# A channel-attention kernel: freed rows of maxima refilled with x, graded last loads, stores in more pieces, another order of reloads

## The chip, the cores and the metric

The kernel runs on one core of one Trainium2 chip; the other cores are idle. The metric is the device time of one execution in microseconds (us), lower is better. A profiled execution also has a span, from its first to its last instruction, about 1.8 us shorter than its time. Medians are over the executions of a kernel.

Engines are named as the profile names them: PE is TensorE, DVE is VectorE, ACT is ScalarE, SP is SyncE. Here SP issues all loads of x and ACT all stores. A "row" below means 128 x 384 bf16 values, one row of 384 channels in each of 128 partitions: 98,304 bytes.

## The reference

```python
# x: (1, 384, 384, 384) bf16; w1: (384, 96); w2: (96, 384)
xf = x.reshape(B, H * W, C)
gap = jnp.mean(xf, 1)                  # mean of each channel over all pixels
gmp = jnp.amax(xf, 1)                  # maximum of each channel over all pixels
h_a = relu(gap @ w1)                   # relu written out for this page
h_m = relu(gmp @ w1)
scale = sigmoid(h_a @ w2 + h_m @ w2)
return x * scale[:, None, None, :]
```

The scale of a channel needs all of x, and the output needs the scale. So x (113.25 MB, 1152 rows) is read once for the sums and maxima, and read again for the product, but for what can stay on the chip.

## The kernel before

The first pass streams x through six slots of SBUF. TensorE adds up the rows, VectorE keeps an accumulator of 11 rows of maxima. When all of x has passed, the last six blocks are still in their slots, and the first 16 rows lie in PSUM. Those 277 rows are not read again.

```python
SLOTS = (44, 44, 44, 44, 44, 41)       # rows in each slot: 261
PSUM_ROWS = 16
ACC_ROWS = 11
HALVES, QUARTERS = 9, 4                # last blocks: nine loaded in halves, four in quarters
FIRST_STORES = ((1, 2, 3, 4, 4, 6, 8, 8, 8), (10, 12, 22))
...
loads = [(0, PSUM_ROWS, 0, 0, PSUM_ROWS)]
for i, (first, n, s) in enumerate(blocks):
    behind = n_blocks - 1 - i
    j = 0
    for m in cut(n, 4 if behind < QUARTERS else 2 if behind < QUARTERS + HALVES else 1):
        loads.append((first, n, s, j, j + m))
        j += m
...
for i, (first, n, s, lo, hi) in enumerate(loads):          # the first pass
    rows = slots[s][:, lo:hi, :]
    m = hi - lo
    nc.sync.dma_start(out=rows, in_=rows_of(xr, first, n)[:, lo:hi, :])
    ...                                                     # sums on TensorE
    for j in range(0 if i else A, m, A):
        k = min(A, m - j)
        nc.vector.tensor_tensor(out=acc[:, 0:k, :], in0=acc[:, 0:k, :], in1=rows[:, j:j + k, :], op=ALU.max)
```

Then comes the turn between the passes: the 11 rows of maxima are halved to one, transposed, reduced, and put through the two small matrix products and the sigmoid.

```python
n = A
while n > 1:
    h = n // 2
    nc.vector.tensor_tensor(out=acc[:, 0:h, :], in0=acc[:, 0:h, :], in1=acc[:, n - h:n, :], op=ALU.max)
    n -= h
...
nc.scalar.activation(out=scale_bc, in_=z_ps, func=ACT.Sigmoid)
```

In the second pass VectorE multiplies a block in its slot, ACT issues its store, and SP reloads the slot with a block of the rest when the store has landed.

```python
while k < len(order):
    first, n, s = order[k]
    pieces = list(firsts.pop(0)) if firsts else [n]
    put(order[k], pieces)              # multiply and store, piece by piece
    k += 1
    fits = [b for b in again if b[1] <= SLOTS[s]]
    if fits:
        ...
        get(b, cut(b[1], 2) if k <= 2 else [b[1]])
        order.append(b)
```

## Time and profile before

| | before |
|---|---|
| median of the first 6 executions | 747.89 us (747.2 to 756.33) |
| span of the profiled one | 746.1 us |
| bytes moved | 312.81 MB |
| last load's bytes end / first store's bytes begin | 268.7 us / 279.1 us |
| halving of the maxima begins / scale ready | 272.0 us / 277.8 us |

From the page of the kernel before. The busy line has one digit for each fortieth of the span, in tenths; the GB/s line is what the transfer engines moved in the same slices. The queue lines give packets, MB and the time of their packets as a share of 16 engines over the span; q1 carries the loads, q10 the stores.

```profile
span 746.1 us, 2405 instructions
...
DMA  9999999999999939999999999999999999999997
GB/s 382 427 430 434 424 435 431 421 428 430 425 429 419 421 159 369 435 433 435 429 450 427 429 435 435 432 424 434 445 435 435 435 423 432 433 437 432 437 424 341
DMA packets 16363, 312.81 MB, mean 419 GB/s; under 512 B 2176, under 2 KB 2528, under 8 KB 4320
...
q1 hardware_dynamic: 10368, 199.27, 62.6%
q10 hardware_dynamic: 5984, 113.40, 35.5%
```

The transfer engines are full except in slice 15, which is the turn, and at the very end. Everything else hides behind them.

The turn, from the timeline of VectorE before. Columns: start and length in us, engine, line, operation, output and inputs, count; in brackets the idle time before it and what ended it.

```profile
263.06 8.94 DVE L153 TENSOR_TENSOR acc<-acc,x_90 128x4224 bf16<-128x4224 bf16 x4
272.03 2.74 DVE L168 TENSOR_TENSOR acc<-acc 128x1920 bf16<-128x1920 bf16 x4
275.43 0.56 DVE L172 TENSOR_REDUCE gT<-bank_a 128x3 bf16<-128x384 bf16 x1 [0.67 <-PE bank_a L171]
276.41 0.29 DVE L175 TENSOR_SCALAR hbc<-bank_a 96x128 bf16<-96x128 f32 x1 [0.42 <-PE bank_a L174]
277.81 9.51 DVE L181 TENSOR_TENSOR x_85<-x_85,scale_bc 128x384 bf16<-128x384 bf16 x9 [1.12 <-ACT scale_bc L177]
```

VectorE goes from the last maxima into the halving without idle time: it is behind the loads. The same stretch in windows (busy time and count of each engine, PE clock, share of the transfer engines, GB/s):

```profile
268.00:269.00 1.00, 0.64 (x8) 0.26 (x2) 1.00 (x1) 0.26 (x1) 0.00 (x0) 0.50 0.32 131
269.00:272.00 3.00, 1.95 (x8) 1.69 (x9) 2.96 (x2) 0.79 (x3) 0.00 (x0) 0.50 0.00 0
272.00:275.00 3.00, 1.95 (x37) 1.47 (x38) 2.63 (x4) 0.45 (x2) 0.00 (x0) 0.50 0.00 0
...
279.00:280.00 1.00, 0.00 (x0) 0.00 (x0) 1.00 (x2) 0.00 (x0) 0.00 (x0) 0.50 0.70 247
```

No byte moves from 269 to 279 us. That is the dead time the change aims at.

The cost of a maximum, from VectorE's groups by form (busy us, mean ns of one, idle before):

```profile
L153 DVE TENSOR_TENSOR acc<-acc,x_85 128x4224 bf16<-128x4224 bf16 x16 | 37.7, 2358 | 2.4 <-DMA x_85<-in_x_dram 1.9
...
L168 DVE TENSOR_TENSOR acc<-acc 128x1920 bf16<-128x1920 bf16 x1 | 1.2, 1159 | 0.0
```

Eleven rows take 2.358 us and five 1.159, so a row costs 0.200 us and an instruction 0.160 us besides. The Trainium skill, "VectorE: DVE Perf Modes", section "The TRN2 errata", says that operations on SBUF pay a fixed cost per instruction, measured there at about 150 cycles of 0.96 GHz; 0.160 us are 153 cycles, so this trace agrees. A piece cut so that it needs one more instruction costs VectorE that much more.

### The profile page before, as it was taken

The numbers are of one execution on the slowest core, as the hardware profiler recorded it, in microseconds if no ns is written. First come the engines' busy times: TensorE is split into PE (matmuls) and PEld (weight loads), VectorE is DVE, ScalarE is ACT, GpSimd is POOL, SyncE is SP. The second block draws the span as 40 slices with busy tenths as digits, with TensorE's granted clock in tenths as the row PEclk, the third lists the DMA queues.
The fourth block names the chain that finished last, engine by engine and source line by source line (L and its number), as shares of the span: only waits on it lengthen the run. The fifth ranks groups of instructions, "written<-read, shape, count | busy, mean of one in ns | idle before, by whom it ended". The sixth has DMA issues, their size and how long they took to land.

```text
span 746.1 us, 2405 instructions
## 1 busy us (share of the span) xinstructions
PE 127.6 (17%) x949; PEld 40.4 (5%) x949; DVE 488.5 (65%) x158; ACT 3.5 (0%) x9; POOL 0.7 (0%) x6
## 2 busy tenths in 40 slices
PE   1554433445445540000000000000000000000000
PEld 0111111111111120000000000000000000000000
DVE  4989999999999989997444434444434444444420
ACT  0000000000000010000000000000000000000000
POOL 0000000000000000000000000000000000000000
PEclk9766766755555555555555555555555555555555
DMA  9999999999999939999999999999999999999997
GB/s 382 427 430 434 424 435 431 421 428 430 425 429 419 421 159 369 435 433 435 429 450 427 429 435 435 432 424 434 445 435 435 435 423 432 433 437 432 437 424 341
DMA packets 16363, 312.81 MB, mean 419 GB/s; under 512 B 2176, under 2 KB 2528, under 8 KB 4320
## 3 DMA queue, kind: packets, MB, share of 16 engines
q1 hardware_dynamic: 10368, 199.27, 62.6%
q10 hardware_dynamic: 5984, 113.40, 35.5%
q8 instruction: 7, 0.11, 0.1%
q14 instruction: 4, 0.03, 0.0%
HBM read 199.41 MB, written 113.25 MB: 419 GB/s over the span
## 4 chain that ended last, share of the span: by engine, by line
another core or an unknown queue 42%; DMA 28%; DVE 24%; SPq 1%; DVEq 1%; issue 0%; PE 0%; ACT 0%
DVE acc L153 21%; DMA x_87<-in_x_dram 9%; DMA x_89<-in_x_dram 7%; DMA out_dram<-x_89 6%; DMA w_sb<-in_w_dram 3%; DMA out_dram<-x_86 2%; DVE x_85 L181 1%; DVE x_86 L181 1%; DMA x_86<-in_x_dram 1%; SPq L199 1%; DVEq L245 1%; DVE acc L168 0%; DVE gT L172 0%; PE bank_a L171 0%
## 5 line engine op out<-in xcount | busy, mean ns | idle before, releaser
L181 DVE TENSOR_TENSOR x_85<-x_85,scale_bc 128x16896 bf16<-128x16896 bf16 (+6 forms) x13 | 45.3, 3537 | 36.2 <-DMA x_85<-in_x_dram 35.1
L181 DVE TENSOR_TENSOR x_86<-x_86,scale_bc 128x16896 bf16<-128x16896 bf16 (+4 forms) x7 | 44.3, 6354 | 33.7 <-DMA x_86<-in_x_dram 32.4
L181 DVE TENSOR_TENSOR x_87<-x_87,scale_bc 128x16896 bf16<-128x16896 bf16 (+1 forms) x5 | 37.4, 7476 | 37.1 <-DMA x_87<-in_x_dram 37.1
L181 DVE TENSOR_TENSOR x_89<-x_89,scale_bc 128x16896 bf16<-128x16896 bf16 x4 | 35.8, 8956 | 32.5 <-DMA x_89<-in_x_dram 32.5
L181 DVE TENSOR_TENSOR x_88<-x_88,scale_bc 128x16896 bf16<-128x16896 bf16 x4 | 35.8, 8956 | 31.7 <-DMA x_88<-in_x_dram 31.7
L181 DVE TENSOR_TENSOR x_90<-x_90,scale_bc 128x15744 bf16<-128x15744 bf16 x4 | 33.4, 8356 | 31.0 <-DMA x_90<-in_x_dram 31.0
L153 DVE TENSOR_TENSOR acc<-acc,x_89 128x4224 bf16<-128x4224 bf16 x20 | 47.2, 2358 | 6.5 <-DMA x_89<-in_x_dram 5.9
L115 PEld LDWEIGHTS <-ones_bf 128*1 128x1 bf16 x900 | 36.5, 111 | 231.2 <-issue 228.3
L153 DVE TENSOR_TENSOR acc<-acc,x_90 128x4224 bf16<-128x4224 bf16 (+3 forms) x20 | 44.2, 2208 | 0.8
L153 DVE TENSOR_TENSOR acc<-acc,x_85 128x4224 bf16<-128x4224 bf16 (+1 forms) x17 | 38.9, 2287 | 2.4 <-DMA x_85<-in_x_dram 1.9
L153 DVE TENSOR_TENSOR acc<-acc,x_88 128x4224 bf16<-128x4224 bf16 (+1 forms) x17 | 39.3, 2311 | 1.5 <-DMA x_88<-in_x_dram 1.0
L153 DVE TENSOR_TENSOR acc<-acc,x_86 128x4224 bf16<-128x4224 bf16 x16 | 37.7, 2358 | 2.6 <-DMA x_86<-in_x_dram 2.1
L153 DVE TENSOR_TENSOR acc<-acc,x_87 128x4224 bf16<-128x4224 bf16 x16 | 37.7, 2358 | 1.4 <-DMA x_87<-in_x_dram 0.9
L115 PE MATMUL bank_a<-x_89,ones_bf 128*1 128x512 bf16 (+2 forms) x171 | 24.5, 600 | 30.2 <-DMA x_89<-in_x_dram 30.2
L115 PE MATMUL bank_a<-x_85,ones_bf 128*1 128x512 bf16 (+1 forms) x150 | 20.8, 588 | 30.9 <-DMA x_85<-in_x_dram 30.9
L115 PE MATMUL bank_a<-x_88,ones_bf 128*1 128x512 bf16 (+2 forms) x144 | 20.4, 590 | 20.9 <-DMA x_88<-in_x_dram 20.9
L115 PE MATMUL bank_a<-x_90,ones_bf 128*1 128x512 bf16 (+3 forms) x159 | 19.3, 523 | 20.8 <-DMA x_90<-in_x_dram 20.8
L115 PE MATMUL bank_a<-x_86,ones_bf 128*1 128x512 bf16 (+1 forms) x138 | 18.9, 587 | 22.5 <-DMA x_86<-in_x_dram 22.5
L115 PE MATMUL bank_a<-x_87,ones_bf 128*1 128x512 bf16 (+2 forms) x138 | 18.5, 566 | 20.8 <-DMA x_87<-in_x_dram 20.8
L149 DVE COPY acc<-x_85 128x4224 bf16<-128x4224 bf16 x1 | 1.3, 1260 | 5.6 <-DMA x_85<-in_x_dram 5.6
L155 DVE COPY kept_ps<-x_85 128x3072 uint32<-128x3072 uint32 x1 | 3.4, 3355 | 0.0
L181 DVE TENSOR_TENSOR x_88<-kept_ps,scale_bc 128x6144 bf16<-128x6144 bf16 x1 | 3.4, 3351 | 0.0
(33 smaller groups left out, 18.4 us busy)
## 6 DMA issues: line engine op xcount, KB each, us to landing
x_89<-in_x_dram SPq DMA_DIRECT2D x6, 4224.0 KB, 34.3
x_85<-in_x_dram SPq DMA_DIRECT2D x5, 4224.0 KB, 34.4
x_87<-in_x_dram SPq DMA_DIRECT2D x5, 4224.0 KB, 34.9
x_88<-in_x_dram SPq DMA_DIRECT2D x5, 4224.0 KB, 34.7
x_90<-in_x_dram SPq DMA_DIRECT2D x5, 3936.0 KB, 34.2
x_86<-in_x_dram SPq DMA_DIRECT2D x4, 4224.0 KB, 36.0
out_dram<-x_87 ACTq DMA_DIRECT2D x4, 4224.0 KB, 74.4
out_dram<-x_88 ACTq DMA_DIRECT2D x4, 4224.0 KB, 73.6
```

The lines of the kernel that those rows point to most:

```text
L115: nc.tensor.matmul(sum_ps[q * QP:q * QP + 1, 0:g * P], lhsT=ones_bf[:, 0:1], rhs=rows[:, k:k + g, q * P:(q + 1) * P], start=(done + k == 0 ...
L149: nc.vector.tensor_copy(out=acc, in_=rows[:, 0:A, :])
L153: nc.vector.tensor_tensor(out=acc[:, 0:k, :], in0=acc[:, 0:k, :], in1=rows[:, j:j + k, :], op=ALU.max)
L155: nc.vector.tensor_copy(out=kept_ps.bitcast(U32), in_=rows.bitcast(U32))
L181: nc.vector.tensor_tensor(out=dst, in0=src, in1=scale_bc.unsqueeze(1).to_broadcast([P, n, C]), op=ALU.mult)
L199: nc.sync.dma_start(out=slots[s][:, j:j + m, :], in_=rows_of(xr, first, n)[:, j:j + m, :])
L245: with _tile.TileContext(nc) as tc:
```

## The change

Its intent: use the dead time and shorten it. Ten of the 11 rows of maxima are spent after the halving; they are filled with x in the turn, so that ten rows fewer are streamed later. Two small tiles are laid over others, which makes room for two more rows in the last slot. The last loads get smaller towards the end, so that less work follows the last of them. The first blocks are stored in more pieces, and the first reload is to wait until two blocks are stored.

```diff
-SLOTS = (44, 44, 44, 44, 44, 41)
+SLOTS = (44, 44, 44, 44, 44, 43)
-HALVES, QUARTERS = 9, 4
-FIRST_STORES = ((1, 2, 3, 4, 4, 6, 8, 8, 8), (10, 12, 22))
+LAST_LOADS = ((22, 22),) * 7 + ((17, 16, 11), (17, 16, 11), (15, 15, 14), (11, 11, 11, 11), (10, 9, 8, 8, 8))
+FIRST_STORES = ((1, 2, 3, 4, 4, 6, 8, 8, 8), (8, 8, 9, 9, 10), (10, 12, 22))
+FIRST_READS = (2, 2)
+LEAD = 2
+ACC_STORES_AT = 3
...
-    left = TOT - PSUM_ROWS
+    head = PSUM_ROWS + A - 1
+    left = TOT - head
...
-    w2_sb = consts.tile([R, C], BF16)
+    scale_bc = consts.tile([P, C], BF16)
+    w2_sb = scale_bc[0:R, :]
+    s_sb = consts.tile([P, P], F32)
+    hbc = s_sb[0:R, :].bitcast(BF16).rearrange("r (t p) -> r t p", t=2)
...
-    loads = [(0, PSUM_ROWS, 0, 0, PSUM_ROWS)]
+    loads = [(0, PSUM_ROWS, 0, 0, PSUM_ROWS), (PSUM_ROWS, A - 1, 1, 0, A - 1)]
...                                     # pieces of the last blocks now from LAST_LOADS
     while n > 1:
         h = n // 2
         nc.vector.tensor_tensor(out=acc[:, 0:h, :], in0=acc[:, 0:h, :], in1=acc[:, n - h:n, :], op=ALU.max)
         n -= h
+        if n > 1 and acc_pieces:
+            continue
+        lo, hi = n, acc_pieces[0][0] if acc_pieces else A
+        nc.sync.dma_start(out=acc[:, lo:hi, :], in_=rows_of(xr, PSUM_ROWS, A - 1)[:, lo - 1:hi - 1, :])
+        acc_pieces.append((lo, hi))
...                                     # put() multiplies and stores acc after three pieces
+        if k == LEAD:
+            read_into(order[k - 1][2])
+            for j in range(k - 1):
+                read_into(order[j][2])
+        elif k > LEAD:
+            read_into(order[k - 1][2])
```

More of the change, by code (lines that the diff above doesn't have):

```diff
@@ L59 @@
         n = min(SLOTS[slot], left)
-        blocks.insert(0, [left - n + PSUM_ROWS, n, slot])
+        blocks.insert(0, [left - n + head, n, slot])
         left -= n
@@ L79 @@
     nc.scalar.dma_start(out=w1_sb, in_=w1.rearrange("(q p) m -> p q m", p=P))
-    w2_sb = consts.tile([R, C], BF16)
+    scale_bc = consts.tile([P, C], BF16)
+    w2_sb = scale_bc[0:R, :]
     nc.scalar.dma_start(out=w2_sb, in_=w2)
+    s_sb = consts.tile([P, P], F32)
+    hbc = s_sb[0:R, :].bitcast(BF16).rearrange("r (t p) -> r t p", t=2)
     gT = consts.tile([P, CQ, 2], BF16)
-    s_sb = consts.tile([P, P], F32)
     acc = consts.tile([P, A, C], BF16)
@@ L96 @@
     hTa_ps = bank_b[0:R, C + 8:C + 9]
-    def cut(n, parts):
-        return [n // parts + (k < n % parts) for k in range(parts)]
-    loads = [(0, PSUM_ROWS, 0, 0, PSUM_ROWS)]
+    loads = [(0, PSUM_ROWS, 0, 0, PSUM_ROWS), (PSUM_ROWS, A - 1, 1, 0, A - 1)]
     for i, (first, n, s) in enumerate(blocks):
-        behind = n_blocks - 1 - i
-        j = 0
-        for m in cut(n, 4 if behind < QUARTERS else 2 if behind < QUARTERS + HALVES else 1):
-            loads.append((first, n, s, j, j + m))
-            j += m
+        left = n
+        for m in LAST_LOADS[i - n_blocks] if i >= n_blocks - len(LAST_LOADS) else (n,):
+            m = min(m, left)
+            loads.append((first, n, s, n - left, n - left + m))
+            left -= m
+        assert left == 0
     n_loads = len(loads)
@@ L155 @@
             nc.vector.tensor_copy(out=kept_ps.bitcast(U32), in_=rows.bitcast(U32))
-    late2 = ctx.enter_context(tc.tile_pool(name="late2", bufs=1))
-    hbc = late2.tile([R, 2, P], BF16)
-    scale_bc = late2.tile([P, C], BF16)
     nc.scalar.mul(out=gT[:, :, 0], in_=gsum_ps, mul=1.0 / HW)
@@ L165 @@
     n = A
+    acc_pieces = []
     while n > 1:
@@ L183, in multiply, with put_acc, put @@
         )
-    def put(block, pieces):
+    def put_acc():
+        for lo, hi in acc_pieces:
+            multiply(acc[:, lo:hi, :], acc[:, lo:hi, :])
+            nc.scalar.dma_start(out=rows_of(orr, PSUM_ROWS, A - 1)[:, lo - 1:hi - 1, :], in_=acc[:, lo:hi, :])
+    def put(block, pieces, acc_at=None):
         first, n, s = block
         j = 0
-        for m in pieces:
+        for i, m in enumerate(pieces):
+            if i == acc_at:
+                put_acc()
             rows = slots[s][:, j:j + m, :]
@@ L193, in put, with cut @@
         assert j == n
+    def cut(n, parts):
+        return [n // parts + (k < n % parts) for k in range(parts)]
     def get(block, pieces):
@@ L203, with read_into @@
     again = sorted(blocks[:n_stream], key=lambda b: -b[1])
-    firsts = list(FIRST_STORES)
-    k = 0
-    while k < len(order):
-        first, n, s = order[k]
-        pieces = list(firsts.pop(0)) if firsts else [n]
-        put(order[k], pieces)
-        k += 1
+    stores, reads = list(FIRST_STORES), list(FIRST_READS)
+    def read_into(s):
         fits = [b for b in again if b[1] <= SLOTS[s]]
@@ L215 @@
             b = (b[0], b[1], s)
-            get(b, cut(b[1], 2) if k <= 2 else [b[1]])
+            get(b, cut(b[1], reads.pop(0) if reads else 1))
             order.append(b)
+    k = 0
+    while k < len(order):
+        put(order[k], stores.pop(0) if stores else (order[k][1],), None if k else ACC_STORES_AT)
+        k += 1
+        if k == LEAD:
[4 more added lines that the diff above has]
+            read_into(order[k - 1][2])
     assert not again
```

## The prediction

> **What bounds the kernel now.** The transfer engines: the forty-slice view has them at 9 tenths in all slices but the turn between the passes (159 GB/s in slice 15) and the end; the page's total is 312.81 MB in 746.1 us. A row (128 x 384 bf16, 98,304 B) costs 0.2276 us: whole 44-row loads land 10.01 us apart in the timeline of TensorE's waits, 432 GB/s. The Trainium skill, "DMA: Bandwidth & Descriptors", section "Bandwidth", gives 435 GB/s as the fabric ceiling; the trace agrees, so only bytes or dead time can go.
>
> The dead time is the turn: in half-microsecond windows the last load's bytes end at 268.7 us and the first store's begin at 279.1. There VectorE is the chain (in the chain of waits without a break from 139.8 to 272.0): it finishes the last 10 rows at 272.0, halves the maxima until 274.8, and the scale is ready at 277.8.
>
> **What the change does.**
>
> 1. Ten spent accumulator rows are loaded with x inside the dead time (five after the first halving, five after the last), and two more rows stay on chip (slot of 43 for 41). Before, 1152 - 16 - 261 = 875 rows were read again outside the turn; after, 863. Twelve rows x 0.2276 = -2.7 us, all on the critical path. Ten rows take 2.3 us plus about 2 us latency, which fits in the turn.
>
> 2. Graded last loads. A maximum costs 0.195 + 0.1998 us per row, gap included (2.36 us for 11 rows, 2.16 for 10, plus 0.035). VectorE gains on the loads only 4 to 5% with 11-row pieces, hardly anything with 17+16+11 (maxima of 11+6, 11+5, 11) or 15+15+14. Following loads and maxima piece by piece with these costs gives an end at 271.9 before (272.0 measured) and 273.0 after: one more block lands whole before the halves begin, and there are more maxima. The shorter last piece (8 rows, 1.76 us against 2.16) is lost; the scale comes LATER: +1.0 us, on the path.
>
> 3. Stores in more small pieces (x_86 in five, x_87 in three). From 284 to 287 us, 8-row stores run near 400 GB/s at a full busy share, against 430: some 50 more such rows cost an estimated +0.6 us.
>
> 4. The first reload waits for two stored blocks. The engines do not starve: VectorE multiplies 8 rows in 1.75 us, their transfer takes 1.9 to 2.0. It moves bytes in time, not their number, and may avoid the dip where loads first mix with small stores (about 376 GB/s from 288 to 300 us): -0.7 us. At the end more than 80 rows of stores are still queued when the last load lands, so nothing waits.
>
> Putting w2 and the hidden rows into other tiles adds no wait that ends last.
>
> **Sum.** -2.7 + 1.0 + 0.6 - 0.7 = -1.8 us.
>
> **Predicted: 746.0 us**, range 743.5 to 748.2. Faster by over 2%: 0.01; within 2%: 0.98; slower by over 2%: 0.01.
>
> **What would show it.** 0.98 MB of loads inside the turn; the last maximum ending at 272.5 to 273.5 and the sigmoid at 278.3 to 279.3; the acc multiplies without a wait of note; full engines from 282 us to the end; first reload near 298 us.
>
> **What would make it wrong.** Step 2 is least certain: if loads land unlike the averages, VectorE may catch up, and the total falls to 744. If the store-only stretch leaves the engines short of work, or the last 31-row block leaves a hole at the end, the gain is lost. The spread of the runs (747.2 to 749.8) is as large as the gain.

## More of the kernel before

Last, a pair of lines that the prediction did not look at and that turned out to matter, from the timeline of the second pass, VectorE and SP. VectorE's multiply starts when a load has landed; SP's next load is issued when a store has landed and its slot is free.

```profile
381.80 8.96 DVE L181 TENSOR_TENSOR x_88<-x_88,scale_bc 128x16896 bf16<-128x16896 bf16 x1 [10.70 <-DMA x_88<-in_x_dram]
...
386.70 0.33 SPq L199 DMA_DIRECT2D x_90<-in_x_dram  x1
```

A load landed at 381.8 us and a store at 386.7, 4.9 us later. The pattern repeats every 20 us to the end of the pass.

## The result, and the profile after

| | before | after |
|---|---|---|
| median (lowest to highest) | 748.06 us (746.97 to 757.97, 20 runs) | 745.56 us (744.98 to 747.21, 10 runs) |
| span of the profiled run | 746.1 us | 743.6 us |
| bytes moved | 312.81 MB | 312.61 MB |
| halving begins | 272.03 us | 273.47 us |
| scale ready (first multiply) | 277.81 us | 279.26 us |
| first store's bytes begin | 279.1 us | 280.6 us |

The ratio of after to before is 0.9949, 95% interval 0.992 to 0.9979. Ratios here are the mean time of one kernel's fast runs over that of the other's of the same rounds, so not quite the ratio of the medians quoted. The gain is real and small: 2.5 us in the medians.

From the page of the kernel after:

```profile
span 743.6 us, 2410 instructions
...
DMA  9999999999999959999999999999999999999998
GB/s 376 428 432 433 430 434 430 422 428 426 430 426 421 421 205 356 414 433 437 435 431 434 432 436 436 436 433 434 432 436 436 436 425 437 434 433 423 438 428 366
DMA packets 17083, 312.61 MB, mean 420 GB/s; under 512 B 2256, under 2 KB 2608, under 8 KB 5552
```

Slice 15 went from 159 to 205 GB/s: the refill is there. The turn in VectorE's timeline after:

```profile
263.90 9.53 DVE L157 TENSOR_TENSOR acc<-acc,x_90 128x3840 bf16<-128x3840 bf16 x5
273.47 2.74 DVE L170 TENSOR_TENSOR acc<-acc 128x1920 bf16<-128x1920 bf16 x4
276.88 0.56 DVE L179 TENSOR_REDUCE gT<-bank_a 128x3 bf16<-128x384 bf16 x1 [0.67 <-PE bank_a L178]
277.85 0.29 DVE L182 TENSOR_SCALAR s_sb<-bank_a 96x128 bf16<-96x128 f32 x1 [0.42 <-PE bank_a L181]
279.26 1.50 DVE L188 TENSOR_TENSOR x_85<-x_85,scale_bc 128x384 bf16<-128x384 bf16 x3 [1.12 <-ACT scale_bc L184]
280.67 2.22 DVE L188 TENSOR_TENSOR acc<-acc,scale_bc 128x1920 bf16<-128x1920 bf16 x2
```

Again VectorE has no idle time before the halving, which now begins 1.4 us later. The acc multiplies follow without a wait: the refill has landed in time. In windows:

```profile
272.00:275.00 3.00, 2.05 (x30) 1.56 (x30) 2.93 (x3) 0.55 (x3) 0.00 (x0) 0.50 0.00 0
275.00:277.00 2.00, 0.50 (x3) 0.40 (x4) 1.26 (x4) 0.00 (x0) 0.00 (x0) 0.50 0.59 148
277.00:279.00 2.00, 0.82 (x4) 0.34 (x3) 0.72 (x2) 0.27 (x1) 0.00 (x0) 0.50 0.79 221
279.00:280.00 1.00, 0.00 (x0) 0.00 (x0) 0.74 (x2) 0.22 (x1) 0.00 (x0) 0.50 0.59 238
```

148 x 2 + 221 x 2 + 238 x 1 kB are 0.98 MB between 275 and 280 us: the ten rows. SP's queue after shows when the refill and the first reload are issued:

```profile
274.66 1.91 SPq L175 DMA_DIRECT2D acc<-in_x_dram  x2
291.46 0.33 SPq L216 DMA_DIRECT2D x_85<-in_x_dram  x1
```

The first reload goes to x_85, the first block's slot, at 291.46 us. So it does not wait for two stored blocks, in spite of the source; in the compiled program the reloads of x_85 stand ahead of those of x_86, the first of which is issued at 312.70 us. And the pair of lines from the second pass after:

```profile
381.11 8.96 DVE L188 TENSOR_TENSOR x_88<-x_88,scale_bc 128x16896 bf16<-128x16896 bf16 x1 [10.90 <-DMA x_88<-in_x_dram]
...
393.48 0.33 SPq L216 DMA_DIRECT2D x_90<-in_x_dram  x1
```

Here the store lands 12.4 us after the load, where it was 4.9 us.

The accounts of the two profiled runs: the first store's bytes begin 1.5 us later. From there to the end it is 467.0 us before (746.1 - 279.1) and 463.0 after (743.6 - 280.6), 4.0 us less. Twelve rows fewer are 12 x 0.2276 = 2.7 us of those. The other 1.3 us lie in the last microseconds: before, the engines trickled until nearly 745 us, in the windows of a microsecond from 742 us at 135, 37 and 12 GB/s; after, there is one such window, of 49 GB/s from 741 us. The trace's records of single packets show what a trickle is. Up to 742.2 us 16 packets run at a time before, at 742.6 three, and from 743.4 on one: one of the 16 transfer engines ends some 2.5 us after most of the others, and the kernel waits for it. That last item is about as large as the spread of one kernel's own runs.

### The profile page after: what moved, and what is told of

It reads as the page before. It is cut to its first block, busy times and chain, and to the rows that moved or that the text cites. A ratio compares the mean times of both kernels' runs of the same rounds, so it can differ in the third digit from the quotient of the medians.

```text
span 743.6 us, 2410 instructions
## 1 busy us (share of the span) xinstructions
PE 127.8 (17%) x943; PEld 40.5 (5%) x943; DVE 489.3 (66%) x167; ACT 3.5 (0%) x9; POOL 0.7 (0%) x6
## 2 busy tenths in 40 slices
DMA packets 17083, 312.61 MB, mean 420 GB/s; under 512 B 2256, under 2 KB 2608, under 8 KB 5552
## 4 chain that ended last, share of the span: by engine, by line
another core or an unknown queue 40%; DVE 35%; DMA 17%; DVEq 1%; issue 1%; SPq 1%; PE 0%; ACT 0%
DVE acc L157 28%; DMA out_dram<-x_89 6%; DMA x_87<-in_x_dram 6%; DMA x_85<-in_x_dram 3%; DMA w_sb<-in_w_dram 2%; DVE x_85 L188 1%; DVEq L269 1%; DVE x_86 L188 1%; DVE x_87 L188 1%; DVE x_89 L188 1%; DVE x_88 L188 1%; SPq L216 1%; DVE acc L170 0%; DVE acc L188 0%
## 5 line engine op out<-in xcount | busy, mean ns | idle before, releaser
L188 DVE TENSOR_TENSOR x_85<-x_85,scale_bc 128x3072 bf16<-128x3072 bf16 (+7 forms) x13 | 42.8, 3338 | 31.4 <-DMA x_85<-in_x_dram 30.3
L188 DVE TENSOR_TENSOR x_90<-x_90,scale_bc 128x16512 bf16<-128x16512 bf16 x4 | 35.0, 8757 | 32.4 <-DMA x_90<-in_x_dram 32.4
L188 DVE TENSOR_TENSOR x_87<-x_87,scale_bc 128x16896 bf16<-128x16896 bf16 (+3 forms) x6 | 36.0, 6022 | 30.0 <-DMA x_87<-in_x_dram 30.0
L157 DVE TENSOR_TENSOR acc<-acc,x_90 128x4224 bf16<-128x4224 bf16 (+3 forms) x21 | 46.3, 2206 | 4.6 <-DMA x_90<-in_x_dram 3.9
L157 DVE TENSOR_TENSOR acc<-acc,x_89 128x4224 bf16<-128x4224 bf16 (+1 forms) x19 | 44.4, 2337 | 3.8 <-DMA x_89<-in_x_dram 3.2
L157 DVE TENSOR_TENSOR acc<-acc,x_86 128x4224 bf16<-128x4224 bf16 (+3 forms) x18 | 40.1, 2225 | 2.6 <-DMA x_86<-in_x_dram 2.0
L157 DVE TENSOR_TENSOR acc<-acc,x_85 128x4224 bf16<-128x4224 bf16 (+1 forms) x17 | 38.9, 2287 | 1.8 <-DMA x_85<-in_x_dram 1.4
L157 DVE TENSOR_TENSOR acc<-acc,x_87 128x4224 bf16<-128x4224 bf16 (+2 forms) x17 | 37.9, 2229 | 1.9 <-DMA x_87<-in_x_dram 1.4
L157 DVE TENSOR_TENSOR acc<-acc,x_88 128x4224 bf16<-128x4224 bf16 (+2 forms) x18 | 38.0, 2114 | 1.5 <-DMA x_88<-in_x_dram 1.0
L119 PE MATMUL bank_a<-x_89,ones_bf 128*1 128x512 bf16 (+2 forms) x162 | 22.7, 589 | 27.0 <-DMA x_89<-in_x_dram 27.0
L119 PE MATMUL bank_a<-x_90,ones_bf 128*1 128x512 bf16 (+3 forms) x165 | 22.5, 577 | 25.7 <-DMA x_90<-in_x_dram 25.7
L119 PE MATMUL bank_a<-x_85,ones_bf 128*1 128x512 bf16 (+1 forms) x150 | 19.6, 560 | 28.0 <-DMA x_85<-in_x_dram 28.0
L119 PE MATMUL bank_a<-x_86,ones_bf 128*1 128x512 bf16 (+3 forms) x147 | 19.9, 574 | 21.9 <-DMA x_86<-in_x_dram 21.9
L119 PE MATMUL bank_a<-x_88,ones_bf 128*1 128x512 bf16 (+2 forms) x138 | 18.9, 582 | 22.1 <-DMA x_88<-in_x_dram 22.1
L119 PE MATMUL bank_a<-x_87,ones_bf 128*1 128x512 bf16 (+3 forms) x138 | 18.9, 581 | 21.6 <-DMA x_87<-in_x_dram 21.6
```

The costliest lines, as they stand in the source:

```text
L119: nc.tensor.matmul(sum_ps[q * QP:q * QP + 1, 0:g * P], lhsT=ones_bf[:, 0:1], rhs=rows[:, k:k + g, q * P:(q + 1) * P], start=(done + k == 0 ...
L188: nc.vector.tensor_tensor(out=dst, in0=src, in1=scale_bc.unsqueeze(1).to_broadcast([P, n, C]), op=ALU.mult)
```

## The experiments

Eleven new kernels ran, and the kernel after once more, all in rounds of five, in three groups of four; all gave correct results. In the summary, "halving" is the start of the halving of the maxima. "Load to store" is the distance from a load's landing to the next store's landing in the second pass, from the same lines as above, over the periods from 350 to 700 us. "Slow loads" counts, in the trace's records of single packets after 340 us, the load packets (one partition of a block, 31,488 to 33,792 bytes) that took over 1.3 us, scaled to 33,792 bytes, where nearly all take 1.251; "excess" is what all load packets took above 1.251 us, as the mean of the 16 transfer engines. These last two columns are counted from the one profiled run, which need not be near the median.

| run | median (lowest to highest), us | ratio to before | halving, us | load to store, us | slow loads | excess, us |
|---|---|---|---|---|---|---|
| before | see groups | 1 | 272.03 | 4.8 to 5.1 | 6 of 2304 | 0.1 |
| after | 745.56 (744.98 to 747.21) | 0.9949 | 273.47 | 12.3 to 12.5 | 5 of 2176 | 0.1 |
| group 1, before 747.74 (746.88 to 756.36) | | | | | | |
| loads_back | 744.13 (743.26 to 747.68) | 0.9954 | 272.37 | 11.5 to 11.7 | 4 of 2175 | 0.0 |
| no_refill | 747.69 (746.63 to 751.11) | 1.0002 | 273.52 | 12.0 to 12.4 | 1 of 2303 | 0.0 |
| refill_only | 752.27 (750.18 to 781.21) | 1.0056 | 272.00 | 1.9 to 3.9 | 299 of 2304 | 7.0 |
| graded_only | 748.61 (747.0 to 749.37) | 1.0005 | 273.08 | 4.8 to 5.0 | 5 of 2304 | 0.1 |
| group 2, before 750.52 (747.03 to 782.11) | | | | | | |
| stores_back | 753.08 (748.28 to 756.84) | 1.0007 | 273.10 | 2.3 to 3.4 | 260 of 2176 | 4.5 |
| refill_slots | 747.13 (746.81 to 749.44) | 0.9939 | 271.80 | 2.5 to 2.6 | 83 of 2176 | 1.1 |
| lead_one | 744.96 (744.25 to 746.26) | 0.9909 | 272.96 | 12.3 to 12.5 | 2 of 2176 | 0.0 |
| refill_stores | 743.60 (743.54 to 743.78) | 0.9887 | 272.10 | 12.0 to 12.5 | 1 of 2288 | 0.0 |
| group 3, before 747.64 (747.38 to 749.16) | | | | | | |
| before_stores | 747.11 (746.33 to 749.61) | 0.9992 | 272.24 | 9.6 to 10.3 | 26 of 2289 | 0.4 |
| reads_whole | 743.75 (743.59 to 744.87) | 0.9945 | 272.25 | 12.0 to 12.5 | 1 of 2288 | 0.0 |
| combined | 744.97 (743.63 to 746.81) | 0.9958 | 272.53 | 12.3 to 12.5 | 2 of 2169 | 0.0 |
| after_again | 745.54 (744.19 to 746.98) | 0.9963 | 273.43 | 12.3 to 12.5 | 21 of 2176 | 0.3 |

The runs of 781.21 and 782.11 us count as slow and are in no ratio, but they are in the medians of the table: over the fast runs alone the median of refill_only is 751.51 us and that of the kernel before in group 2 is 749.48. The kernel before itself runs unevenly: in group 2 four of its eleven runs took 756 to 758 us, in group 3 none. Its ratio in group 2 flatters the others, so kernels are best compared within a group by their own times. Where the text compares across groups, the chips differ too; the medians of the kernel before in groups 1 and 3 are 0.1 us apart.

The halving has a spread of its own. It begins at 271.80 to 272.53 us in the eight kernels with even last loads (mean 272.2) and at 272.96 to 273.52 in the six with graded ones (mean 273.3); a single difference of a few tenths says nothing.

### loads_back: the even grading of the last loads in the kernel after

```diff
-LAST_LOADS = ((22, 22),) * 7 + ((17, 16, 11), (17, 16, 11), (15, 15, 14), (11, 11, 11, 11), (10, 9, 8, 8, 8))
+LAST_LOADS = ((22, 22),) * 8 + ((11, 11, 11, 11),) * 4
```

> The kernel after, with only its grading of the last loads put back to the even one (eight blocks in halves, four in quarters of 11). My theory: the uneven pieces cost VectorE more maxima than they save, so here the last maximum of the stream ends at about 271.9 us (273.4 in the kernel after), the sigmoid about 1.5 us earlier, and the total is about 1.3 us lower, near 744.3. The rival (the shorter last piece of 8 rows helps the turn) has the last maximum at 273.4 or later and the total at 745.6 or above.

Measured: 744.13 us, and in VectorE's timeline:

```profile
272.37 2.74 DVE L170 TENSOR_TENSOR acc<-acc 128x1920 bf16<-128x1920 bf16 x4
```

That is 1.1 us earlier than in the kernel after, and the median is 1.4 us lower than that of the kernel after in another group. In group 3 the same edit, with LEAD = 1 (combined against after_again), lowers it by only 0.6 us with overlapping ranges, so the times alone do not give the size. The grading delays the turn, as the theory said; the intent of a shorter last piece is not met, because VectorE is still behind when that piece lands.

### graded_only: the grading alone in the kernel before

```diff
-HALVES, QUARTERS = 9, 4
+LAST_LOADS = ((22, 22),) * 7 + ((17, 16, 11), (17, 16, 11), (15, 15, 14), (11, 11, 11, 11), (10, 9, 8, 8, 8))
...                                     # and the loop that reads it, as in the change
```

> The kernel before with only the graded last loads. My theory: the last maximum ends at about 272.9 us instead of 272.0 and the total rises by about 0.9 us, near 749.0. The rival, the intent of the grading (a shorter last piece shortens the turn), has the last maximum earlier than 272.0 and the total below 748.

Measured: 748.61 us against 747.74, and the halving at 273.08 us against 272.03. Both are near what was expected. The ratio, 1.0005 with an interval from 0.9981 to 1.0028, cannot tell so small a difference; the timeline can. VectorE runs 111 maxima here against 106; five more at 0.195 us each, the prediction's fixed cost with the gap, are 1.0 us.

### no_refill: the kernel after, its ten rows streamed like the rest

```diff
-    head = PSUM_ROWS + A - 1
+    head = PSUM_ROWS
...
-        nc.sync.dma_start(out=acc[:, lo:hi, :], in_=rows_of(xr, PSUM_ROWS, A - 1)[:, lo - 1:hi - 1, :])
-        acc_pieces.append((lo, hi))
```

> The kernel after without the ten rows loaded into the spent accumulator rows: they are streamed again like the others, 873 rows instead of 863 outside the turn. My theory: 10 rows x 0.2276 = 2.3 us more of saturated transfer, total near 747.8, with the turn itself unchanged (last maximum near 273.4, first store bytes near 280.6). The rival (the loads in the turn only push the first stores back, so they bring nothing) has the total unchanged within 0.5 us and the first stores earlier.

Measured: 747.69 us, 2.1 us above the kernel after (2.3 expected), with the halving at 273.52 us as in the kernel after (273.47). The refill is worth its rows. The first store's bytes begin at 280.6 us with the loads in the turn and without them, so the loads do not push the stores back.

### refill_only: the refill alone in the kernel before

```diff
+    head = PSUM_ROWS + A - 1
+    left = TOT - head
...                                     # and the loads into acc, put_acc(), as in the change
```

> The kernel before with only the refill of ten accumulator rows added (slot of 41, even last loads, first stores and reload order as before). My theory: 10 rows fewer in the saturated part, so 2.3 us less than before, near 745.8, with the last maximum still near 272.0. If the gain of the whole change came from another part, this stays at 748.

Measured: 752.27 us, 4.5 us slower than before (751.51 and 3.8 over the fast runs), where 2 us faster were expected. The turn is as it should be (halving at 272.00 us), so the loss is later. The queues of the second pass, 345 to 700 us, first of the kernel before, then of refill_only:

```profile
DMA packets 5233, 153.46 MB, mean 432 GB/s; under 512 B 577, under 2 KB 577, under 8 KB 640
...
q10 hardware_dynamic: 2623, 77.99, 50.9%
q1 hardware_dynamic: 2609, 75.46, 49.3%
```

```profile
DMA packets 5092, 150.78 MB, mean 425 GB/s; under 512 B 561, under 2 KB 561, under 8 KB 561
...
q1 hardware_dynamic: 2539, 75.15, 50.9%
q10 hardware_dynamic: 2552, 75.62, 49.4%
```

Both are full, but refill_only moves 425 GB/s instead of 432. The stores (q10) move as much per share as before (1.53 MB per percent in both). The loads (q1) do not: 1.53 MB per percent before, 1.48 here. In the records of single packets, 299 load packets are slow, up to 2.9 us for what takes 1.251, and the excess is 7.0 us per engine in the mean. The profiled run took 753.02 us. The author took the expected 745.8 plus 7.0, 752.8, for the whole account, but that agreement is in part luck: two kernels below with the same rows and no slow packets take 743.6 and 743.75 us, not 745.8. Against the profiled run of one of them (reads_whole, span 741.9) the span of 751.2 is 9.3 us longer. The 7.0 us are most of it. Most of the rest is the end, where the engines no longer finish together: 16 packets run at a time until about 745.5 us and eight or fewer from 746.6 to 749.9, while reads_whole has 16 until 739.9 and ends by 740.8. The slow packets come in bursts, about one a period, and two thirds of them start within 4 us of both a load's and a store's landing. The timeline of refill_only there:

```profile
386.62 8.96 DVE L188 TENSOR_TENSOR x<-x,scale_bc 128x16896 bf16<-128x16896 bf16 x1 [11.14 <-DMA x<-in_x_dram]
...
388.51 0.33 SPq L213 DMA_DIRECT2D x<-in_x_dram  x1
```

The store lands 1.9 us after the load, where it was 4.9 us before and 12.4 us after. From this came theory A, tested next: the time depends on how far the ends of loads and stores lie apart in the second pass, and this distance is set by the first stores and reloads and then kept for the whole pass. Theory C was that the slot of 41 rows makes the slowness.

### stores_back: the kernel after without the second block's five pieces

```diff
-FIRST_STORES = ((1, 2, 3, 4, 4, 6, 8, 8, 8), (8, 8, 9, 9, 10), (10, 12, 22))
+FIRST_STORES = ((1, 2, 3, 4, 4, 6, 8, 8, 8), (10, 12, 22))
```

> The kernel after, with only the second block's stores put back to whole pieces (x_86 in 10, 12, 22 as before, then whole blocks). Theory A, from the slow second pass of refill_only: there a load's last packets and a store's last packets fall within 3 us of each other in every period, and the load packets that follow are slow (13% of them over 1.3 us, 7.0 us of excess per engine in all); the kernel after is spared because its extra store pieces part the two ends by 7 us or more. Then this kernel is near refill_only: load packets slow, rate of the second pass near 425 GB/s, total 749 to 752. Theory B (small store pieces only cost, about 0.6 us): total about 745.0 and 433 GB/s. Theory C (slowness came of the 41-row slot): about 745.

Measured: 753.08 us (748.28 to 756.84), load to store 2.3 to 3.4 us, 260 slow load packets, 427 GB/s in the second pass. Theory A holds, with a median 1.1 us above its range; B and C fail: the rival that small store pieces only cost had 745. In the same group lead_one, which has the five pieces and differs otherwise only in LEAD, took 744.96 us. So one line of store pieces, which also cuts the third block's store, is worth some 8 us here.

### refill_slots: refill and 43-row slot, the rest as before

```diff
-LAST_LOADS = ...
-FIRST_STORES = ((1, 2, 3, 4, 4, 6, 8, 8, 8), (8, 8, 9, 9, 10), (10, 12, 22))
-LEAD = 2
+LAST_LOADS = ((22, 22),) * 8 + ((11, 11, 11, 11),) * 4
+FIRST_STORES = ((1, 2, 3, 4, 4, 6, 8, 8, 8), (10, 12, 22))
+LEAD = 1
```

> The refill and the 43-row slot alone, with the even last loads, the first stores and the reload order of the kernel before. Theory A: the ends of loads and stores fall together as in refill_only, so a slow second pass and 748 to 751 in spite of the lowest traffic and the early turn. Theory C (the 41-row slot makes the slowness): 743.5 to 744.5, and 433 GB/s.

Measured: 747.13 us. That lies between the two numbers. Its distance is 2.5 us and it has 83 slow packets, but only 1.1 us of excess in the mean. The profiled run, which is the slowest with 749.44 us, shows that this mean understates the loss. Its last microseconds, in the columns of the windows above:

```profile
739.00:740.00 1.00, 0.00 (x0) 0.00 (x0) 0.00 (x0) 0.00 (x0) 0.00 (x0) 0.50 0.60 254
740.00:741.00 1.00, 0.00 (x0) 0.00 (x0) 0.00 (x0) 0.00 (x0) 0.00 (x0) 0.50 0.31 131
...
743.00:744.00 1.00, 0.00 (x0) 0.00 (x0) 0.00 (x0) 0.00 (x0) 0.00 (x0) 0.50 0.32 135
```

One engine moves 33,792 bytes in 1.251 us, 27.0 GB/s; 131 to 135 GB/s are five engines. In the records of single packets, too, 16 run at a time until 739.3 us and about five from 740.1 to 744.1; the last ends at 746.4. So the delay fell on some five engines, and the kernel waited for these. In the mean of all 16 it looks small. That the slow packets are what delayed these five is likely and not shown, since the records do not name the engine. The median misses theory A's range by 0.9 us; C, with 744.5 at most, is not met either. combined, in group 3, is this kernel with the five store pieces, and took 744.97 us without slow packets.

### lead_one: the kernel after with the first reload not held back

```diff
-LEAD = 2
+LEAD = 1
```

> The kernel after, with only the first reload no longer held back (LEAD of 1). In the compiled program the reload instructions of the first two blocks stand in the same order in both; only which of the two reloaded blocks is multiplied first differs. So I expect no difference: 745.6 within 0.5 us, no slow load packets, first reload at about 291 us. The rival (holding back the first reload gains something) has 747 or more.

Measured: 744.96 us, no slow packets, the same distance. The first reload is issued at 290.94 us, 0.5 us before that of the kernel after (291.46), and the halving is 0.5 us earlier too. So LEAD = 2 does not hold the first reload back in the compiled program, and nothing is gained that these runs can tell.

### refill_stores: refill_only with the five pieces of stores

```diff
-FIRST_STORES = ((1, 2, 3, 4, 4, 6, 8, 8, 8), (10, 12, 22))
+FIRST_STORES = ((1, 2, 3, 4, 4, 6, 8, 8, 8), (8, 8, 9, 9, 10), (10, 12, 22))
```

> refill_only with only the kernel after's second block of stores in five pieces (and the third in 10, 12, 22). Theory A: the ends of loads and stores come apart, the slow load packets vanish, and what was expected of refill_only comes out: about 745.8 (last maximum near 272.0, second pass at 432 GB/s or more). Theory C (41-row slot makes the slowness): still slow, 750 or more.

Measured: 743.60 us, with all six runs within 0.24 us of each other, distance 12 us, one slow packet. With the slot of 41 rows, so theory C falls. It is even 2 us below what was expected. The expectation started from the time of the kernel before, whose profiled run loses about 2 us to the late engine at its end; here 16 packets run at a time until 739.9 us and the last ends by 740.8.

### before_stores: the five pieces alone in the kernel before

```diff
-FIRST_STORES = ((1, 2, 3, 4, 4, 6, 8, 8, 8), (10, 12, 22))
+FIRST_STORES = ((1, 2, 3, 4, 4, 6, 8, 8, 8), (8, 8, 9, 9, 10), (10, 12, 22))
```

> The kernel before with only the kernel after's second block of stores in five pieces; no refill, slot of 41, even last loads. Theory A (the ends of loads and stores come apart, so no run falls into slow load packets): all runs within about 1 us of each other, near 746 (10 rows x 0.2276 = 2.3 us above the 743.6 of refill_stores), against a kernel before that spreads from 747 to 757. The rival (the pieces help only together with the refill, or cost 0.6 us by their size): spread as before, median 748 or more.

Measured: 747.11 us (746.33 to 749.61). This is a miss: the median is 1 us above what was expected and the runs are not closer together than those of the kernel before on this chip (747.38 to 749.16). The distance is about 10 us, and the profiled run, which was the slowest one with 749.61 us, has 26 slow packets. The pieces alone give little.

### reads_whole: refill_only with the first two reloads whole

```diff
-            get(b, cut(b[1], 2) if k <= 2 else [b[1]])
+            get(b, [b[1]])
```

> refill_only with only the first two reloads whole instead of in halves: the first then waits for all of the first block's stores, some 4 us longer, and nothing else changes. It moves the ends of loads against the ends of stores without touching the store pieces. Theory A says the time follows that distance: if the trace shows the ends of a load and of the store nearest to it over 4 us apart, no slow packets and about 746; if still within 3 us, slow packets and 750 or more. The rival (it is the small store pieces that matter, not the distance) says slow, 750 or more, whatever the distance.

Measured: 743.75 us (743.59 to 744.87), 8.5 us below refill_only (7.8 over fast runs), by taking a cut out. refill_only ran on another chip, in group 1; each is compared with the kernel before of its own group by the ratios, 0.9945 and 1.0056. In the timeline:

```profile
378.66 8.96 DVE L188 TENSOR_TENSOR x<-x,scale_bc 128x16896 bf16<-128x16896 bf16 x1 [10.76 <-DMA x<-in_x_dram]
...
390.77 0.33 SPq L213 DMA_DIRECT2D x<-in_x_dram  x1
```

and in the queues of its second pass:

```profile
DMA packets 5215, 153.84 MB, mean 433 GB/s; under 512 B 592, under 2 KB 592, under 8 KB 592
```

The distance went from about 2 to 12 us, the slow packets went, and the rate is 433 GB/s. No store piece was touched, so the rival that the small pieces themselves matter falls. This is the strongest of the tests: the two edits, store pieces and whole reloads, share no line, and both moved the distance from about 2 to 12 us. What they have in common besides the distance, if anything, was not looked for.

### combined and after_again: putting the parts together

```diff
-LAST_LOADS = ((22, 22),) * 7 + ((17, 16, 11), (17, 16, 11), (15, 15, 14), (11, 11, 11, 11), (10, 9, 8, 8, 8))
+LAST_LOADS = ((22, 22),) * 8 + ((11, 11, 11, 11),) * 4
-LEAD = 2
+LEAD = 1
```

> What the runs so far point to: refill, slot of 43 and five store pieces of the kernel after, with the even last loads and LEAD of 1. Last maximum near 271.9, no slow load packets, 2 rows less than refill_stores: 743.1, and lower than the kernel after of the same rounds by 1.5 to 2.5 us.

> The kernel after once more, unchanged, as the measure for the run before it on the same chip: 745.0 to 746.0, no slow load packets, spread of 2 us or less.

Measured: combined 744.97 us (743.63 to 746.81), the kernel after again 745.54 us (744.19 to 746.98). The combination was expected at 743.1 and is a miss by 1.9 us; it is 0.6 us below the kernel after, with overlapping ranges. On the same chip reads_whole took 743.75 us, 1.8 us below the kernel after and 3.9 us below the kernel before; all of its five runs lie under the median of after_again. It is the best version of that group, and it is the kernel before with the refill and without the cut of the first reloads. The profiled run of after_again, 746.98 us, has 21 slow packets and its transfers trickle out at 160, 37 and 12 GB/s in the last three windows of a microsecond; from 742.9 us on a single packet runs at a time. So the distance of 12 us does not remove slow packets in every run.

## Why the prediction was right

The time, 745.56 us, was predicted at 746.0. Two of its four terms were right. The other two were wrong, and that they nearly cancelled each other in the sum (+0.6 and -0.7) is luck.

1. **The refill and the two rows, -2.7 us: right.** The ten rows are in the turn (0.98 MB from 275 to 280 us), the multiplies of acc do not wait, and without the refill the kernel takes 2.1 us more where 10 x 0.2276 = 2.3 was expected. The 0.5 us of the other two rows no run shows apart.

2. **The graded loads, +1.0 us: right in cause and, in the turn, in size.** The halving begins at 273.47 us instead of 272.03, 1.4 us later where 1.0 was predicted; with even loads it is back at 272.37. In the kernel before the grading alone moves it to 273.08. Over all the kernels with and without the grading the difference is 1.1 us. What it costs in the total the times do not settle (0.6 to 1.4 us). The account was VectorE's: it is behind the loads, gains on them only through full instructions of 11 rows, and uneven pieces add instructions of 0.160 us fixed cost.

3. **Smaller store pieces, +0.6 us: wrong in sign.** The step asked what the pieces cost while they are being stored. What they do is to set how the loads and stores of the whole second pass fall in time. Without them the kernel after takes 753.08 us, 8.1 more than lead_one of the same group. That is a loss which the refill would have brought and the pieces avert: in the kernel before, which has few slow packets, they alone give 0.5 us that the ratio cannot tell from nothing (0.9978 to 1.0006).

4. **The first reload waits, -0.7 us, first reload near 298 us: wrong.** It was issued at 291.46 us. The step was read from the source and not from the order of instructions in the compiled program, where the first block's reloads still stand first. Undoing it changes nothing that these runs can tell (744.96 against 745.56 on another chip).

The sum missed a further 1.3 us that the profiled run of the kernel after gained in the last microseconds, because no engine ended as late as in the kernel before; such a difference appears between runs of one kernel too, so this part of the gain is luck of the run as far as is shown. And the prediction named as the danger that the runs' spread is as large as the gain. It took this spread for noise; part of what it saw is likely the second pass of the kernel before, which has its ends 4.9 us apart. But none of its runs of 756 us was profiled, so that these had slow load packets is argued, not shown.

What the runs show: slow load packets account for most of the loss of refill_only (7.0 us in the mean of the engines) and of stores_back (4.5 us); what is left lies mostly at the end, where some engines finish later than others. They came in number (83 to 299) in all three kernels whose ends lie within 4 us of each other, and no kernel with 4.8 us or more had over 26. Two unrelated edits that moved the ends apart removed them. So it is shown that the first stores and reloads decide over the slow packets. That they do so through the distance is the reading that fits the fourteen profiled runs, but no run has a distance between 5.1 and 9.6 us. What stays open: why a load packet is slow there, why 2.5 us of distance brought few slow packets in refill_slots and many in stores_back, and why combined is not below reads_whole although it moves two rows less.

## What to carry to other kernels

In a kernel bound by its transfers, a change of the first few transfers can set a rhythm of loads and stores that is then kept for hundreds of microseconds; look at where loads and stores end, and at the time of single packets, before explaining a small gain or loss by the bytes. Look at the last microseconds too: the kernel ends with its latest transfer engine, and a mean over the engines hides a delay of a few. Before making pieces smaller to shorten a tail, follow the engine that does the work piece by piece with its fixed cost per instruction: if it is behind, small pieces only put it further behind. And read a change of order from the compiled program's instructions, not from the source.

## What the Trainium skill lacked or had wrong

- "DMA: Bandwidth & Descriptors", section "Queues, rings and completion order", says that an engine alternates between the rows it has work for, packet by packet; the records agree (store and load packets of 33,792 bytes in turn, 1.251 us each, with q1 and q10 at half of the time each). It has nothing on what this costs when a load and a store end together: load packets of up to 2.9 us, 7.0 us of excess per engine in refill_only, and 425 instead of 432 to 433 GB/s over the second pass.
- The same page, "Specifications", gives about 27 GiB/s per engine; 33,792 bytes in 1.251 us are 27.0 GB/s, so 16 engines make the 432 to 433 GB/s seen here, which its fabric ceiling of 435 GB/s fits and 27 GiB/s, which is 29.0 GB/s, does not.
- No page says how much the cutting of a load costs when only loads run, queued one behind the other: in the first pass of the kernel before 44 rows took 10.01 us whole, 10.09 us in halves (2 x 5.045) and 10.23 us in quarters (4 x 2.557).
- "VectorE: DVE Perf Modes", section "The TRN2 errata", advises operands of 512 elements or more to dilute the fixed cost; at 1,920 elements it is still 0.160 of 1.159 us here, and five extra instructions in the last five blocks were enough to delay the turn by about 1.1 us.
